# Gate bias and q spreads ahead of load issues on GpSimd, an even split of the k sort copies, MoE pieces from unit 16, and the last four q heads loaded behind the first row scatters

## The chip, the cores and the metric

The kernel runs on one core of a Trainium2 chip. A core has five engines that each run their own list of instructions in order: TensorE (PE, matrix multiplies; its weight loads are shown as PEld), VectorE (DVE), ScalarE (ACT), GpSimd (POOL, which here also issues the large loads and the indirect scatters) and SyncE (SP, which here only issues transfers). They meet through semaphores. The metric is the device time of a run in microseconds: 243.31 us as the median of three runs (243.28 to 244.02). The profiled execution has a span of 207.0 us from its first to its last instruction; times within the profile are counted from the start of that span.

## The reference

Two parts are computed, one behind the other. First a block attention with sorted blocks, for 4 batches of 8 heads, 768 positions and 64 columns per head:

```
P = sort_net (8 x 8 for each head), 5 times: exp, rows to sum 1, columns to sum 1
k_sorted, v_sorted = P applied to the 8 blocks of 96 rows of k and v
scores = q_block . k_sorted_block^T / 8    (96 x 96 per block)
attn_out = softmax(scores) . v_sorted_block
```

The result is laid out as x, 3072 rows of 512 columns. Then a mixture of experts with one expert for each row:

```
logits = x @ w_gate + modality_bias[modality_id];  e = argmax;  p = softmax(logits)[e]
out = p * (relu(x @ w1[e]) @ w2[e])       w1: 512 x 1024, w2: 1024 x 512, 8 experts
```

## The kernel before, in words

**Attention.** Heads and batches are packed into two groups g (two batches each). A group has 16 units, numbered u = 0 to 15 for group 0 and 16 to 31 for group 1: one head (u modulo 8), of two batches at once, for four of the eight blocks. For each group the blocks of k and v are sorted by matmuls with a block diagonal matrix made of P (`make_bd`); `sort_k` (L361) and `sort_v` (L371) do it in jobs, and each job's PSUM tile is copied out by ScalarE or VectorE. Which of the two is chosen by `pick` (L344): it keeps a running sum of costs for both (`busy`, charged through `use`) and gives a copy to the one with the smaller sum. The tile of a job comes from one of three pools, named "mi" (four tiles), "sc" and "op" (one tile each, twice as wide); the list `kinds` (L763) names the pool for each of the jobs of group 0. Group 1's jobs are spread over units 8 to 15.

q is loaded by head, laid side by side for two batches by a copy (`spread_q`, L123, two copies for each pair of heads, on GpSimd for group 0 and on VectorE for group 1), and transposed by TensorE (`prep_q`: tq). A unit then is `scores` (sc), `expo` (ScalarE's exp), `av` (op, and VectorE's division by the row sums into xb). `prep_s` and `prep_q` prepare q for units u + 3 and u + 2.

**Gate.** Eight units finish 768 rows of x, a stage m (0 to 3). `gate_T` transposes xb (gt), `gate_L` multiplies with w_gate (lg) and adds into lacc; its first part adds biasm, the bias of each row, which `gate_bias` (L327, four GpSimd instructions) makes. `choose` takes the argmax, `place` (L491) works out the slot of each row and sends the rows with eight indirect scatters from GpSimd to a scratch in DRAM (xs_scratch), and `table_x` works out which slots are full and loads them, transposed, on SyncE's queue.

**Experts.** Two experts' weights fit (w01). The MoE work is a list of pieces: a quarter of the first product for 256 rows (`mL1`, hp) or half of the second (`mL2`, yp, followed by an indirect scatter of rows to the output from GpSimd). `run_pieces(n)` puts the next n pieces into the order, if their rows have been asked for. `pace` (L881) says how many pieces a unit takes: none before unit 17, then one or two. After the units the rest follows.

**Order.** The order is written out by hand: what is emitted first stands first in its engine's list, and nothing behind a waiting instruction can overtake it. `at1(u, ...)` puts work in the middle of unit u (ahead of `av`), `at2(u, ...)` at its end. On GpSimd the sequence is: loads of q, k and v of group 0; spread of heads 0 and 1; loads of k of group 1; tables of the gate (`home_map`, `gate_w`, L323); spread of heads 2 and 3; load of v of group 1 (it waits until v of group 0 has been read); spread of heads 4 and 5; q of group 1 (`load_q`, L116) and the first expert's weights, in turn; small constants; spread of heads 6 and 7; the gate bias; then the rows of stage 0, the second expert's weights (`late_w1`, which waits for the transposed load of the second slot), and so on. `home_pick` (L214) is a chain of 13 small VectorE instructions that is emitted ahead of the sort of k.

Of the kernel before, what the change touches and what calls it, by code (L numbers as in the profile page):

```python
# [17 lines left out]
def kernel(  # L18
# [13 lines left out]
    nc = tc.nc  # L32
# [58 lines left out]
    def q_in(g, hh):  # L91
        base = q_in1 if g else v_sb[1].rearrange("p x d -> p (x d)")
        return base[:, hh * 3072:(hh + 1) * 3072]
# [15 lines left out]
    def load_k(g, part):  # L109
        cs = slice(part * RW // 2, (part + 1) * RW // 2)  # L110
        nc.gpsimd.dma_start(out=k_raw[:, cs], in_=k_src[g * 128:(g + 1) * 128, cs])

    def load_v(g):
        nc.gpsimd.dma_start(out=v_in, in_=v_src[g * 128:(g + 1) * 128])

    def load_q(g, h0, nh):  # L116
        t = q_in(g, h0 // 4).rearrange("p (r h f) -> p r h f", r=2, h=4)
        z = h0 % 4
        for par in range(2):
            nc.gpsimd.dma_start(out=t[:, par, z:z + nh], in_=q[2 * g + par, h0:h0 + nh]  # L120
                                .rearrange("h (p t) d -> p h (t d)", t=6))

    def spread_q(g, hq, eng=None):  # L123
        t = q_in(g, hq // 2).rearrange("p (r h t d) -> p r h t d", r=2, h=4, t=6)
        il = q_il[hq % 2].rearrange("p (h t r d) -> p h t r d", h=2, t=6, r=2)
        for z in range(2):
            (eng or nc.vector).tensor_copy(il[:, z], t[:, :, (hq % 2) * 2 + z].rearrange("p r t d -> p t r d"))  # L127
# [62 lines left out]
    def perm_mult(dst, srcs, nm):  # L190
        eng = nc.gpsimd
        tmp = small.tile([128, 4, E, E], FP32, tag="ptmp", name=f"ptmp{nm}")
        a = bass.AP(tensor=srcs.tensor, offset=srcs.offset, ap=[srcs.ap[0], srcs.ap[1], [0, E], srcs.ap[2]])
        p_ = bass.AP(tensor=perm.tensor, offset=perm.offset, ap=[perm.ap[0], [0, 4], perm.ap[1], perm.ap[2]])
        eng.tensor_tensor(tmp, a, p_, ALU.mult)
        for w in (4, 2):
            eng.tensor_tensor(tmp[:, :, :, 0:w], tmp[:, :, :, 0:w], tmp[:, :, :, w:2 * w], ALU.add)
        eng.tensor_tensor(dst.rearrange("p r (e o) -> p r e o", o=1), tmp[:, :, :, 0:1], tmp[:, :, :, 1:2], ALU.add)
# [32 lines left out]
    def tq_pe(u):  # L231
        h = u % 8
        src = q_il[(h // 2) % 2].rearrange("p (h t f) -> p h t f", h=2, t=6)[:, h % 2]
        tp = mipsum.tile([128, 6, 128], BF16, tag="mi", name=f"tq{u}")
        for t in range(6):
            nc.tensor.transpose(tp[:, t], src[:, t], ident)  # L236
        tq[u] = tp

    def tq_out(u, eng):
        g, h = u // 16, u % 8  # L240
        qT = qTb[g][:, h * 768:(h + 1) * 768].rearrange("p (i t r) -> p i t r", i=NB, t=6)
        eng(qT, tq.pop(u).rearrange("p t (i r) -> p i t r", r=16))
# [55 lines left out]
    def home_map():  # L298
        nc.vector.tensor_tensor_scan(cs_, ones8, oth, 0.0, ALU.mult, ALU.add)
        nc.vector.scalar_tensor_tensor(cs_, cs_, 1.0, oth, ALU.add, ALU.mult)  # L300
        nc.vector.tensor_tensor(cs_, cs_, ohB, ALU.add)
        hb = bass.AP(tensor=cs_.tensor, offset=cs_.offset, ap=[cs_.ap[0], [0, E], cs_.ap[1]])
        nc.vector.tensor_tensor(perm, hb, sF8.broadcast_to([128, E, E]), ALU.is_equal)
        perm_mult(BTp, BT, "b")
        nc.gpsimd.tensor_copy(etab, BTp[0:1, 3])
# [6 lines left out]
    def mod_rows():  # L312
        src = modI.rearrange("b (r t w) -> b t r w", r=16, t=6)[:, :, :, 0]
        nc.gpsimd.tensor_copy(modB, src)
# [8 lines left out]
    def gate_w():  # L323
        perm_mult(wgf, wg_sb, "w")
        nc.gpsimd.tensor_copy(wgp, wgf)

    def gate_bias():  # L327
        nc.gpsimd.tensor_scalar(modN, modF, -1.0, 1.0, ALU.mult, ALU.add)

        def bb(r):  # L330
            t = BTp[0:BLK, r]
            return bass.AP(tensor=t.tensor, offset=t.offset, ap=[t.ap[0], [0, NTL], t.ap[1]])
        tmp = small.tile([BLK, NTL, E], FP32, tag="btmp", name="btmp")
        nc.gpsimd.tensor_tensor(biasm, modF.broadcast_to([BLK, NTL, E]), bb(1), ALU.mult)
        nc.gpsimd.tensor_tensor(tmp, modN.broadcast_to([BLK, NTL, E]), bb(0), ALU.mult)
        nc.gpsimd.tensor_tensor(biasm, biasm, tmp, ALU.add)
# [3 lines left out]
    def use(act=0.0, dve=0.0):  # L340
        busy[0] += act
        busy[1] += dve

    def pick(act, dve):  # L344
        top = max(busy)
        for z in range(2):
            busy[z] = max(busy[z], top - 3.0)
        z = 0 if busy[0] + act <= busy[1] + dve else 1
        busy[z] += (act, dve)[z]
        return z == 0  # L350
# [28 lines left out]
    def jobs(g, kinds):  # L379
        res, c0, d0 = [], 0, 0  # L380
        for kd in kinds:
            if c0 < BLK:
                res.append((sort_k, g, c0, kd))
                c0 += 8 if kd == "mi" else 16
            else:
                res.append((sort_v, g, d0, kd))
                d0 += 4 if kd == "mi" else 8
        assert c0 == BLK and d0 == D
        return res
# [3 lines left out]
    def unit(u):  # L393
        return u // 16, (u // 8) % 2, u % 8
# [6 lines left out]
    def prep_q(u):  # L401
        if 2 <= u < 32 and not (u // 8) % 2:
            tq_pe(u)
            tq_out(u, nc.scalar.copy if pick(0.8, 0.56) else nc.vector.tensor_copy)
# [23 lines left out]
    def av(u):  # L428
        g, hf, h = unit(u)
        xt = xb[(u // 8) % 2]  # L430
        op = opsum.tile([128, 2, 512], FP32, tag="op", name=f"op{u}")
        ov = op[:, :, 0:4 * (D + 1)].rearrange("p r (j x) -> p r j x", x=D + 1)
        for par in range(2):
            for j in range(4):
                i = hf * 4 + j
                c0 = (par * 4 + j) * BLK
                nc.tensor.matmul(ov[:, par, j], attnT[u % 2][:, c0:c0 + 128],  # L437
                                 v_sb[g][0:BLK, par * 64 + h * 8 + i, 0:D + 1], start=True, stop=True)
        rs = small.tile([BLK, 2, 4, 1], FP32, tag="rs", name=f"rs{u}", bufs=2)
        nc.vector.reciprocal(rs, ov[0:BLK, :, :, D:D + 1])  # L440
        nc.vector.tensor_tensor(xt[:, :, h * D:(h + 1) * D].rearrange("p (r j) d -> p r j d", r=2),  # L441
                                ov[0:BLK, :, :, 0:D], rs.broadcast_to([BLK, 2, 4, D]), ALU.mult)
        use(dve=0.92)
# [171 lines left out]
    def zero_block():  # L615
        ins = nc.sync.dma_start(out=xs_dram[ZR:ZR + PR].rearrange("(t p) w -> p t w", t=2), in_=zsrc2)
        in_xs_group(ins.ins)
        pads.append(ins.ins)
# [125 lines left out]
    m_, s_, o_ = "mi", "sc", "op"  # L744
# [15 lines left out]
    use(dve=0.5)  # L760
    home_pick()
    mod_rows()
    kinds = [s_, o_] + [m_] * 8 + ([m_] * 4 + [o_]) * 2 + [m_] * 4  # L763
    g0 = jobs(0, kinds)
    for f, g, x0, kd in g0[:10]:
        f(g, x0, kd)
# [3 lines left out]
    load_k(1, 0)  # L770
    load_k(1, 1)
    home_map()
    gate_w()
    spread_q(0, 1, nc.gpsimd)
    use(dve=-busy[1], act=-busy[0])
    for n, (f, g, x0, kd) in enumerate(g0[10:]):
        f(g, x0, kd)
# [2 lines left out]
            expo(1)  # L780
    load_v(1)
    spread_q(0, 2, nc.gpsimd)
    load_q(1, 0, 4)
    load_w(0, parts=(0,))
    load_q(1, 4, 4)
    load_w(0, parts=(1,))
    make_upper_triangular(nc, maskUT, val=1.0, diag=False)
    nc.gpsimd.iota(zpad.bitcast(I32)[:, Dm // 2:Dm // 2 + 1], pattern=[[0, 1]], base=SKIP, channel_multiplier=0)
    zero_block()
    prep_q(2)  # L790
    av(0)
    prep_q(3)

    st = {"tab": -1, "x": 0, "l1": 0, "done": 0, "pos": 0}

# [21 lines left out]
    def at1(u, f, *a):  # L817
        A1.setdefault(u, []).append((f, a))

    def at2(u, f, *a):  # L820
        A2.setdefault(u, []).append((f, a))
# [7 lines left out]
    for m in range(4):  # L829
        for c in range(4):  # L830
            u = 8 * m + 2 * c + 3
# [5 lines left out]
                at1(u, gate_L, m, c)  # L837
        if m < 3:
            at1(8 * m + 9, choose, m)
    at2(2, lambda: (spread_q(0, 3, nc.gpsimd), gate_bias()))  # L840
    at2(3, make_bd, 1)
    at2(4, late_consts)
    k_at = [8] * 3 + [9] * 3 + [10] * 4 + [11] * 2
# [1 line left out]
    for u, (f, g, x0, kd) in zip(k_at + v_at, jobs(1, [m_] * 28)):  # L845
        at2(u, f, g, x0, kd)
    for m in range(3):
        at2(8 * m + 9, place, m)
        at2(8 * m + 11, table_x, m)
    at2(12, late_w1)  # L850

    PIPE = 6
# [13 lines left out]
    def run_pieces(n):  # L866
        for _ in range(n):
            if st["pos"] >= len(pieces):
                return
            f, a = pieces[st["pos"]]  # L870
            if (f is mL1 and a[0] >= st["x"]) or (f is last_L1 and SL >= st["x"]):
                return
            f(*a)
            if f is mL1 and a[1] == 3:
                st["l1"] = a[0] + 1
            if f is mL2 and a[1] == 1:
                st["done"] = a[0] + 1
            x_try()
            st["pos"] += 1

    def pace(u):  # L881
        return (0, 0) if u < 17 else (1, u % 2)

    for u in range(2, 32):
        p1, p2 = pace(u)
# [10 lines left out]
            f(*a)  # L896
    run_pieces(1)
    av(31)
    run_pieces(1)
    gate_T(3, 3)  # L900
    run_pieces(1)
    gate_L(3, 3)
    choose(3)
    run_pieces(1)
    place(3)
    run_pieces(1)
    table_x(3)
    run_pieces(1000)
    assert st["pos"] == len(pieces)
# [74 lines left out]
```

The softmax here doesn't subtract the row's maximum and nothing guards it: scores larger than these inputs give would overflow.

## Time and profile before

| engine | busy us | share of the span |
|---|---|---|
| TensorE, matmuls | 166.8 | 81% |
| TensorE, weight loads | 121.8 | 59% |
| VectorE | 102.1 | 49% |
| ScalarE | 92.6 | 45% |
| GpSimd | 83.5 | 40% |

The share of an engine is a mean over stages that differ: up to about 40 us the loads and the two sorts set the pace, then the units, and from 81 us the units together with the MoE pieces. The profile's page shows the span in 40 slices of 5.2 us, in which a digit is the busy share in tenths; "PEclk" is the clock that TensorE was granted. The order of time shows each instruction with its start, its length, its engine, its line, what it writes and reads, and in brackets how long its engine stood idle before it and what ended that. The bulk of the traffic is 23.10 MB on GpSimd's queue; 27.35 MB are read from memory and 10.52 MB written. Loads of f32 are turned into bf16 on the way.

### The profile page before, as it was taken

To read this page: it belongs to the slowest core of one execution; us is meant where nothing else is said; L and a number is where in the kernel's file an instruction comes from. 1 tells how busy PE (TensorE), PEld (TensorE's weight loads), DVE (VectorE), ACT (ScalarE), POOL (GpSimd) and SP (SyncE) were. 2 spreads that over 40 slices of the span, in tenths; PEclk is the share of its full clock that TensorE was granted. 3 is DMA by queue.
4 is the path that set the end of the run, shared out by engine and by line. 5 is a ranking of instruction groups with operands and counts; after the bars stand their busy time and mean duration, and the time that the engine had idled before them with its cause. 6 is when DMAs were issued, how large, how long until landed. Compare 5 with 4: busy or idle time off the path is not lost.

```text
span 207.0 us, 5130 instructions
## 1 busy us (share of the span) xinstructions
PE 166.8 (81%) x2034; PEld 121.8 (59%) x2045; DVE 102.1 (49%) x333; ACT 92.6 (45%) x148; POOL 83.5 (40%) x118
## 2 busy tenths in 40 slices
PE   6395497438899998999978999889999999999100
PEld 2135496327698887768657586648676767654000
DVE  5969377255484866864638453572222322223000
ACT  2035368325575797759435674434232223232000
POOL 7901377930007603177241773257631313132300
PEclk9859679755555799999999999999999999999955
DMA  4999999999993326998550226963577321212200
GB/s 54 207 228 205 194 221 196 204 186 211 205 190 81 88 54 57 165 181 215 152 153 3 77 80 184 177 172 110 165 186 187 83 103 51 101 55 101 62 2 0
DMA packets 30160, 27.66 MB, mean 134 GB/s; under 512 B 18831, under 2 KB 25775, under 8 KB 29872
## 3 DMA queue, kind: packets, MB, share of 16 engines
q0 software_dynamic: 11792, 23.10, 51.0%
q1 hardware_dynamic: 18336, 4.16, 11.3%
q8 instruction: 18, 0.29, 0.6%
q14 instruction: 14, 0.11, 0.2%
HBM read 27.35 MB, written 10.52 MB: 183 GB/s over the span
## 4 chain that ended last, share of the span: by engine, by line
PE 60%; issue 10%; POOL 9%; DVE 9%; DMA 4%; ACT 2%; POOLq 0%; DVEq 0%
PE yp L706 20%; PE hp L683 18%; PE gt L450 4%; DMA kvb<-in_k_dram 4%; PE sc L418 3%; PE lg L456 3%; PE op L437 3%; PE ka L366 3%; DVE xb L441 2%; POOL q_il L127 2%; PE va L375 2%; POOL q_in L120 1%; ACT v_sb L353 1%; PE tq L236 1%; PE ypl L736 1%
## 5 line engine op out<-in xcount | busy, mean ns | idle before, releaser
L683 PE MATMUL hp<-xT,w 128*128 128x256 bf16 x384 | 47.3, 273 | 0.1
L527 POOL DMA_INDIRECT xs_scratch<-xb,dest x32 | 29.6, 926 | 38.8 <-issue 37.9
L697 POOL DMA_INDIRECT out_dram<-kvb,idg x25 | 24.5, 982 | 42.9 <-DVE kvb L695 22.0
L683 PEld LDWEIGHTS <-w 128*128 128x128 bf16 x384 | 36.1, 98 | 7.4
L424 ACT ACTIVATE attnT<-sc 96x768 bf16<-96x768 f32 x32 | 25.9, 808 | 10.4 <-PE sc L418 10.1
L441 DVE TENSOR_TENSOR xb<-op,rs 96x512 bf16<-96x512 f32 x32 | 22.0, 686 | 1.2
L706 PE MATMUL yp<-w,qT 128*128 128x512 bf16 x91 | 22.3, 380 | 0.3
L706 PE MATMUL yp<-w,hT 128*128 128x512 bf16 x90 | 21.9, 380 | 0.3
L693 ACT ACTIVATE kvb<-yp,idg 128x512 f32<-128x512 f32 x14 | 9.6, 687 | 20.5 <-PE yp L706 20.5
L695 DVE TENSOR_SCALAR kvb<-yp,idg 128x512 f32<-128x512 f32 x10 | 7.5, 751 | 19.1 <-PE yp L706 17.2
L437 PE MATMUL op<-v_sb,attnT 96*128 96x65 bf16 x256 | 14.9, 206 | 0.7 <-DVE xb L441 0.4
L677 ACT ACTIVATE hT<-hp 128x512 bf16<-128x512 f32 x17 | 10.1, 594 | 11.5 <-PE hp L683 11.2
L450 PE MATMUL gt<-ident,xb 96*128 96x96 bf16 x128 | 9.4, 225 | 7.2 <-DVE xb L441 6.8
L677 ACT ACTIVATE qT<-hp 128x512 bf16<-128x512 f32 x15 | 9.0, 597 | 12.4 <-PE hp L683 12.1
L706 PEld LDWEIGHTS <-hT 128*128 128x128 bf16 x96 | 9.0, 98 | 9.0
L706 PEld LDWEIGHTS <-qT 128*128 128x128 bf16 x96 | 9.1, 98 | 9.0
L437 PEld LDWEIGHTS <-attnT 96*128 96x128 bf16 x256 | 12.3, 106 | 2.8 <-DVE xb L441 0.6
L418 PE MATMUL sc<-qT,kT 64*128 64x96 bf16 (+1 forms) x256 | 12.8, 226 | 1.3 <-ACT kT L353 0.7
L236 PE MATMUL tq<-ident,q_il 128*128 128x128 bf16 x96 | 9.2, 242 | 5.7 <-POOL q_il L127 5.7
L375 PE MATMUL va<-bd,kvb 128*128 128x128 bf16 x128 | 13.8, 278 | 0.0
L366 PE MATMUL ka<-bd,kvb 128*64 128x64 bf16 x384 | 10.0, 220 | 4.3 <-issue 2.0
L375 PEld LDWEIGHTS <-kvb 128*128 128x128 bf16 x128 | 12.8, 191 | 0.3
(179 smaller groups left out, 225.6 us busy)
## 6 DMA issues: line engine op xcount, KB each, us to landing
w<-in_moe_w_dram POOLq DMA_DIRECT2D x4, 1024.0 KB, 8.3
kvb<-in_k_dram POOLq DMA_DIRECT2D x4, 768.0 KB, 9.6
kvb<-in_v_dram POOLq DMA_DIRECT2D x2, 1536.0 KB
q_in<-in_q_dram POOLq DMA_DIRECT2D x4, 384.0 KB, 21.4
xs_scratch<-zpad SPq DMA_DIRECT2D x3, 258.0 KB, 3.3
v_sb<-in_q_dram POOLq DMA_DIRECT2D x4, 192.0 KB, 4.1
v_sb<-in_q_dram POOLq DMA_DIRECT2D x2, 384.0 KB, 21.5
xs_scratch<-xb,dest POOLq DMA_INDIRECT x32, 2.4
```

Source lines behind the costliest of these rows:

```text
L366: nc.tensor.matmul(acc[par * 64:(par + 1) * 64, z], k_raw[:, (c0 + z) * D:(c0 + z + 1) * D], bd[g][:, par * 64:(par + 1) * 64], start=True ...
L375: nc.tensor.matmul(acc[:, z], v_cols[:, d0 + z], bd[g], start=True, stop=True)
L418: nc.tensor.matmul(sc[0:m, par, j * BLK:(j + 1) * BLK], kT[g][rows, x0:x0 + m], qT[rows, i], start=True, stop=True)
L424: mark[0] = nc.scalar.activation(attnT[u % 2][:, 0:8 * BLK].rearrange("p (r f) -> p r f", r=2), sc_tiles.pop(u)[0:BLK, :, 0:4 * BLK], ACT. ...
L437: nc.tensor.matmul(ov[:, par, j], attnT[u % 2][:, c0:c0 + 128], v_sb[g][0:BLK, par * 64 + h * 8 + i, 0:D + 1], start=True, stop=True)
L441: nc.vector.tensor_tensor(xt[:, :, h * D:(h + 1) * D].rearrange("p (r j) d -> p r j d", r=2), ov[0:BLK, :, :, 0:D], rs.broadcast_to([BLK, ...
L450: nc.tensor.transpose(tp[:, t], xb[m % 2][:, t, c * 128:(c + 1) * 128], ident[:BLK, :BLK])
L527: ins = nc.gpsimd.indirect_dma_start(out=xs_dram, out_offset=bass.IndirectOffsetOnAxis(ap=dest[:, t:t + 1], axis=0), in_=xt.bitcast(I32)[: ...
L677: mark[0] = nc.scalar.activation(dst, src, ACT.Relu)
L683: nc.tensor.matmul(hp[:, f], w_at(s, c * F + (2 * j + f) * 128, 128), xT_b[s % NX][:, c], start=(c == 0), stop=(c == 3))
L697: ins = nc.gpsimd.indirect_dma_start(out=out, out_offset=bass.IndirectOffsetOnAxis(ap=idg[:, t, 0:1], axis=0), in_=y, in_offset=None, boun ...
L706: nc.tensor.matmul(yp, hT_b[s % 2][:, fc, t * 128:(t + 1) * 128], w_at(s, 4 * F + fc * Dm, Dm), start=(fc == 0), stop=(fc == 7))
```

## The change

The change moves work in the hand-written order and alters none of the results.

- The cost sum of VectorE is charged 1.6 us more before the sort of k of group 0, and the wide "op" job stands sixth instead of second in the list, so that ScalarE and VectorE get five copies each, where ScalarE had six and VectorE four. It is meant to take account of home_pick, which VectorE works off first.
- On GpSimd the spread of heads 2 and 3 goes ahead of `gate_w`, and the gate bias and the spread of heads 6 and 7 go ahead of the load issues of q and of the weights, whose data is needed later.
- The last four q heads of group 1 are no longer loaded between the halves of the weights, but behind the scatters of stage 0, at the end of unit 10.
- Pieces begin in unit 16 instead of 17. In the tail three calls take two pieces in place of one, and the placing of stage 2 moves from the end of unit 25 into unit 26.

```diff
-    kinds = [s_, o_] + [m_] * 8 + ([m_] * 4 + [o_]) * 2 + [m_] * 4
+    use(dve=1.6)
+    kinds = [s_] + [m_] * 4 + [o_] + [m_] * 4 + ([m_] * 4 + [o_]) * 2 + [m_] * 4
...
     home_map()
+    spread_q(0, 1, nc.gpsimd)
     gate_w()
-    spread_q(0, 1, nc.gpsimd)
...
     load_v(1)
     spread_q(0, 2, nc.gpsimd)
+    gate_bias()
+    prep_q(2)
+    av(0)
+    prep_q(3)
+    spread_q(0, 3, nc.gpsimd)
     load_q(1, 0, 4)
     load_w(0, parts=(0,))
-    load_q(1, 4, 4)
     load_w(0, parts=(1,))
...
-    prep_q(2)
-    av(0)
-    prep_q(3)
...
-    at2(2, lambda: (spread_q(0, 3, nc.gpsimd), gate_bias()))
...
     for m in range(3):
-        at2(8 * m + 9, place, m)
+        if m == 2:
+            at1(26, place, m)
+        else:
+            at2(8 * m + 9, place, m)
         at2(8 * m + 11, table_x, m)
+    at2(10, load_q, 1, 4, 4)
     at2(12, late_w1)
...
     def pace(u):
-        return (0, 0) if u < 17 else (1, u % 2)
+        return (0, 0) if u < 16 else (1, u % 2)
...
     run_pieces(1)
     av(31)
-    run_pieces(1)
+    run_pieces(2)
     gate_T(3, 3)
     run_pieces(1)
     gate_L(3, 3)
     choose(3)
-    run_pieces(1)
+    run_pieces(2)
     place(3)
-    run_pieces(1)
+    run_pieces(2)
     table_x(3)
```

## The prediction

> **What bounds the kernel now.** I read the page first. TensorE is busy for 81% of the span, and the chain that ended last is 60% TensorE, so most of the span is TensorE's. What can be won cheaply is therefore where TensorE stands still or runs at half clock. In the page's 40 slices (5.2 us each) both show at one place:
>
> ```profile
> PE   6395497438899998999978999889999999999100
> PEclk9859679755555799999999999999999999999955
> DMA  4999999999993326998550226963577321212200
> ```
>
> In the seventh slice PE still has 7 tenths, then 4 and 3; the granted clock falls in the eighth and is at half for five slices from the ninth, while PE is back at 8 and 9 tenths. DMA is full for twelve slices. The list of waits names the causes:
>
> ```profile
> DVE lacc L462 <- POOL biasm L336: 6.0, 1, 6.0
> ...
> PE gt L450 <- DVE xb L441: 6.8, 5, 3.5
> ...
> PE tq L236 <- POOL q_il L127: 5.7, 2, 3.2
> ```
>
> The columns are total us, times and longest. VectorE waits once, for 6.0 us, for the gate bias that GpSimd makes. Now the order of time on GpSimd and TensorE there (start, length):
>
> ```profile
> 32.84 1.60 POOL L127 COPY q_il<-v_sb 128x768 bf16<-128x768 bf16 x2
> 34.37 1.50 POOL L120 DMA_DIRECT2D q_in<-in_q_dram  x2
> 35.86 0.76 POOL L638 DMA_DIRECT2D w<-in_moe_w_dram  x1
> 36.59 1.51 POOL L120 DMA_DIRECT2D q_in<-in_q_dram  x2
> 38.05 0.93 POOL L640 DMA_DIRECT2D w<-in_moe_w_dram  x1
> ...
> 39.61 1.58 POOL L127 COPY q_il<-v_sb 128x768 bf16<-128x768 bf16 x2
> ...
> 42.65 0.72 POOL L336 TENSOR_TENSOR biasm<-biasm,btmp 96x256 f32<-96x256 f32 x1
> ```
>
> ```profile
> 37.51 0.42 PE L437 MATMUL op<-v_sb,attnT 96*128 96x65 bf16 x8
> 40.48 0.82 PE L236 MATMUL tq<-ident,q_il 128*128 128x128 bf16 x6 [2.55 <-POOL q_il L127]
> 41.23 0.50 PE L418 MATMUL sc<-qT,kT 64*128 64x96 bf16 x8
> 45.23 0.82 PE L450 MATMUL gt<-ident,xb 96*128 96x96 bf16 x8 [3.49 <-DVE xb L441]
> ```
>
> GpSimd spends 34.37 to 39.0 on issuing loads and only then spreads the last q heads and makes the bias. TensorE waits 2.55 us for the spread. Then it waits 3.49 us for xb of unit 3, which VectorE could have made from 37.9 (its matmuls ended) but makes at 44.48, because the add of the bias (43.40) stands ahead of it. Its matmuls before the gap take 0.42 us, those after it 0.62 for the same work. The next fact is at the other end, the first rows of the MoE:
>
> ```profile
> 61.83 1.05 POOL L527 DMA_INDIRECT xs_scratch<-xb,dest  x1 [15.12 <-issue]
> ...
> 81.12 0.85 POOL L638 DMA_DIRECT2D w<-in_moe_w_dram  x1 [9.64 <-DMA xT<-xs_scratch]
> ```
>
> ```profile
> 73.39 1.36 SPq L650 DMA_TRANSPOSE xT<-xs_scratch  x1
> ```
>
> The first row scatter starts at 61.83, the first transposed load at 73.39, which with the page's median 3.4 us has landed at 76.8, 15.0 us after the first scatter. The first hp matmul starts at 81.15 and stands only behind the code's own order (unit 17); from there to the last matmul at 192.3 TensorE has 95% of the time.
>
> **What the Trainium skill says.** "TensorE: Matmul & The Clock Gate", What's actually happening: the clock is either full or half, set by free-running windows of 3.4 us, half after an idle one, full after a busy one. The trace agrees on states and grid: read us by us, the clock changes at 8.5, 15.3, 22.1, 29.0, 39.2 and 69.9, all on one grid of 3.41 us. But the window that lost it (35.8 to 39.2) had TensorE busy 2.06 us of 3.4, and the one before kept it with 2.44; so "idle" is too strong, and the border lies between. Windows at half clock with 3.34 and 3.19 busy did not bring it back. Same page, Architectural detail: VectorE and ScalarE take instructions strictly in order, GpSimd too. The trace agrees: xb above. "DMA: Bandwidth & Descriptors", Queues, rings and completion order: an engine works off one queue in ring order and takes turns between queues. The trace agrees with the first half: v_sb loads issued at 5.5 to 8.3 landed 21.5 us later, behind k and v. How a Pool load and a SyncE transpose share the engines no row here shows.
>
> **The change, part by part.**
> 1. Bias and last spread ahead of the load issues. The spread of heads 4 and 5 ends at 34.44 as before. The bias takes 43.37 − 41.18 = 2.19 us, so it is there at 36.6; the gate logits are there at 37.2. The 6.0 us wait goes to nothing. The last spread's first half (0.8 us) ends at 37.4; its transposes come up at 37.93. The 2.55 wait goes too. With VectorE free at 37.4: add 0.2, group 1's sort matrix 0.9, xb 0.9, so xb at 39.2 and the gate transpose there instead of at 45.23: **−6.0 us**. What the moved issues delay is hidden: the 1.5 MB of v issued at 32.25 keep the engines full to about 40 (at 200 GB/s), and q and w issued at 38.2 instead of 34.4 queue behind it.
> 2. The clock. TensorE does not stand still, so the window to 39.2 gains the transposes and scores of 0.68 us, 2.7 of 3.4, more than the 2.44 that kept the clock. From the gate transpose (45.23) to the sort of group 1 (54.82) are 9.6 us now. At full clock the rows shrink to about 0.63 (0.82 to 0.52, 0.62 to 0.41, 0.50 to 0.34); 8.0 us busy would save 3.0, but xb chains fill some: bounds 0 and 3.0, I take **−2.5**. From 54.82 to 69.9 TensorE is busy 14.7 us at half clock; all of it at full saves 5.4, and ScalarE with 7.4 of 10 us busy cannot follow that far; bounds 0 and 5.4, I take the middle, **−2.7**. Unit 16 then comes 11.2 us early.
> 3. First pieces a unit earlier, and the last four q heads behind the first scatters. Rows leave 9.3 us earlier (6.0, 2.5, and 0.8 of the 2.7 that lie ahead of them): first scatter 52.5, first rows at 67.5. Unit 16's scores go from 78.71 to 67.5: the first piece comes up just as its rows land. But the q load of 0.79 MB is now issued at 62.3 behind eight scatters of 1.2 us, moves for 3.9 us at 200 GB/s, and shares engines with the transposes. It delays the rows by 0 (turns) to 3.9 us (all ahead): **+2.0**. On GpSimd two issues (1.5 us) come ahead of the second expert's w, which waits for rows at that time anyway: nothing. The heads are used for unit 20, prepared in unit 17, at 69 or later; they land at 67 or so: nothing.
> 4. Two pieces at a time in the tail. TensorE stands still 0.68 and 0.70 us at 133.5 and 135.5 and slows around: 0 to 1.4, I take **−0.7**. The later scatter (unit 26 rather than 25) and two more output scatters ahead of the last rows cost nothing: these rows are at 151 (147.58 and 3.4), and some 16 pieces of about 1.75 us lie between the new last scatter and their first use.
> 5. Even k sort evacuations: VectorE goes from 4 to 5 copies, ScalarE from 6 to 5, and home_pick, which keeps VectorE until 18.76, no longer holds a 16-column job. TensorE waits 1.34 us for it and then 1.96 us for nothing shown (inside one job, which this edit can't cure). Bounds 0 and 1.9; **−0.5**. The spread of heads 2 and 3 ahead of gate_w: not waited for today, nothing.
>
> Sum: −6.0 −2.5 −2.7 +2.0 −0.7 −0.5 = −10.4. The timed runs stand some 36 us above the span (243.3 against 207.0) and I carry the difference over one for one: 243.3 − 10.4 = **232.9 us**.
>
> **The rivals.** *Clock lost again.* Units 6 and 7 have no q transposes left; a window then holds some 2.4 us busy, on the border. If it goes at 42.6 or 46.0, step 2 is −1.5 and the group 1 sort runs as now: −6.0 −1.5 +0.1 −0.7 −0.5 = −8.6: 234.7 (rows with the load's 2.0 at 71.3, unit 16 at 71.2). For: the narrow border, and that 3.3 us busy did not bring it back. Against: xb comes sooner and packs units. *Only the standstill goes.* The window to 39.2 loses the clock as before and later waits move into units 5 to 9, so steps 2, 4 and 5 bring nothing: −6.0: 237.3. *Everything earlier, nothing waits.* The q load slips between the transposes (step 3 costs 0), and steps 4 and 5 bring their upper bounds: −6.0 −2.5 −2.7 −1.4 −1.9 = −14.5: 228.8. For: rows at 67.5 and unit 16 move together. *Slower.* The late q load lands after unit 17's spread and VectorE, in order, stops; rows and second expert slip behind it; TensorE cools, and units 16 to 21, some 16 us, run at half speed. Half speed costs up to 0.6 of 16, 9.6 us, the wait 3.9: 13.5 against 11.2 + 1.2 won: 244.4. For: the only new wait that can stop three engines. Against: the load has 5 us to land and DMA is at 2 to 3 tenths there.
>
> **How the numbers follow.** Forecast 42%; clock lost again 33%; only the standstill 8%; everything earlier 12%; slower 5%. The range has to hold forecast, clock lost and part of each neighbour: step 3's 0 to 3.9 puts ±2 on the forecast, step 2's bounds 3; 228.5 to 237.5 leaves out the slow case and the tails of the −6.0 and −14.5 cases. Faster 0.94, within 0.3% 0.02, slower 0.04.
>
> **What would show it.** Right: no wait of VectorE on biasm, TensorE's idle between 37.9 and 45 under 1 us, clock full in the ninth slice, first scatter at 52 to 54, first hp at 67 to 71. Step 2 wrong: the clock at half again before the group 1 sort. Step 3 wrong: hp's first wait on xT over 4 us, or VectorE waiting on q_in at L127. It would be wrong as a whole if the bias, in its new place, came later than 37.2 because GpSimd waits for load_v's release longer than until 32.25.

## The result, and the profile after

The changed kernel took 236.81 us (median of four runs, 235.57 to 238.71), the kernel before 243.52 us beside it: a ratio of 0.9729, with a 95% interval of 0.9658 to 0.9799. The forecast was 232.9 us, its range 228.5 to 237.5, so direction and range held. The experiments show that the sum behind the number was wrong in three terms which partly cancelled, and that the gain depends on the chip.

One thing has to be known before two pages are compared. The page of before, with its span of 207.0 us, and the 243.3 us of its timed runs are not the same situation. The kernel before took 206.0 and 206.2 us on two of the chips used below, and 245.0 and 245.1 us on two others. The page of the changed kernel is from a chip of the long kind, its span is 233.9 us. Two of the pages below, of the changed kernel in the second group and of the later rows in the third, are from executions 0.8% and 0.5% longer than the median of their runs. The slices of the changed kernel's page (5.8 us each) show what the short pages don't have:

```profile
PE   6573988695289899229989129999659999999400
...
PEclk9799599757559999857999758999959999999965
DMA  5999999999396696242111255404436431211200
```

There are four holes in TensorE's row, at slices 11, 17 and 18, 23 and 24, and 29 and 30, and the clock falls in or behind each. The list of waits says who stood still (total us, times, longest):

```profile
ACT attnT L424 <- remote: 19.6, 3, 9.2
...
PE sc L418 <- ACT attnT L424: 15.7, 5, 8.9
...
PE lg L456 <- issue: 5.4, 1, 5.4
...
PE tq L236 <- POOL q_il L127: 2.9, 1, 2.9
```

"Remote" means that no row of the profile ended the wait. This page holds 1,110 records of landed transfers, the pages of the short kind some 1,700, so the row may also be one that was not recorded. The order of time puts the holes beside the row scatters of the four stages. For stage 2, GpSimd's last rows and ScalarE:

```profile
133.54 0.91 POOL L527 DMA_INDIRECT xs_scratch<-xb,dest  x1 [0.30 <-issue]
134.76 1.00 POOL L697 DMA_INDIRECT out_dram<-kvb,idg  x1 [0.30 <-issue]
136.06 0.98 POOL L697 DMA_INDIRECT out_dram<-kvb,idg  x1 [0.30 <-issue]
```

```profile
137.85 0.81 ACT L424 ACTIVATE attnT<-sc 96x768 bf16<-96x768 f32 x1 [9.19 <-remote]
```

The scores that this exp reads were done at 128.6, the scatters ran from 125.0 to 137.0, and ScalarE goes on 0.8 us after the last.

On GpSimd the change does what it was meant to do: VectorE's wait for biasm is gone from the list, the one wait left for q_il is at 9.6 us, before the sort, and the places that were shown of before now read

```profile
32.18 1.60 POOL L127 COPY q_il<-v_sb 128x768 bf16<-128x768 bf16 x2
...
35.23 0.72 POOL L336 TENSOR_TENSOR biasm<-biasm,btmp 96x256 f32<-96x256 f32 x1
35.90 1.58 POOL L127 COPY q_il<-v_sb 128x768 bf16<-128x768 bf16 x2
37.44 1.60 POOL L120 DMA_DIRECT2D q_in<-in_q_dram  x2
39.03 0.75 POOL L638 DMA_DIRECT2D w<-in_moe_w_dram  x1
39.77 0.91 POOL L640 DMA_DIRECT2D w<-in_moe_w_dram  x1
```

```profile
37.87 0.35 PE L418 MATMUL sc<-qT,kT 64*128 64x96 bf16 x8 [0.27 <-ACT attnT L424]
38.53 0.51 PE L450 MATMUL gt<-ident,xb 96*128 96x96 bf16 x8 [0.31 <-DVE xb L441]
...
42.63 0.41 PE L437 MATMUL op<-v_sb,attnT 96*128 96x65 bf16 x8
43.44 0.80 PE L456 MATMUL lg<-wgp,xTg 128*96 128x8 bf16 x8 [0.40 <-DVE xTg L353]
44.18 0.50 PE L418 MATMUL sc<-qT,kT 64*128 64x96 bf16 x8
44.61 0.62 PE L437 MATMUL op<-v_sb,attnT 96*128 96x65 bf16 x8
```

The second gate transposes start at 38.53 instead of 45.23. But in the last line the same matmuls (op) take 0.62 us where they had taken 0.41: the granted clock is at half again from 43.3, before the sort of group 1 (47.0). The first scatter leaves at 54.02 (61.83 in the page of before, which is of the short kind), the first transposed load is issued at 69.72 and the first piece starts at 78.92 (81.15). Of the 7.8 us won at the scatter 2.2 are left at the first piece. On this chip the hole at slice 11 lies between the two; how much of the loss is the late q load needs the experiments.

### The profile page after: what moved, and what is told of

The parts are those of the page before. It is cut to its first block, busy times and chain, and to the rows that moved or that the text cites. A ratio compares the mean times of both kernels' runs of the same rounds, so it can differ in the third digit from the quotient of the medians.

```text
span 233.9 us, 5147 instructions
## 1 busy us (share of the span) xinstructions
PE 170.7 (73%) x2045; PEld 123.5 (53%) x2045; DVE 102.3 (44%) x333; ACT 93.0 (40%) x148; POOL 83.6 (36%) x118
## 4 chain that ended last, share of the span: by engine, by line
PE 59%; DVE 14%; another core or an unknown queue 9%; issue 6%; ACT 3%; POOL 1%; POOLq 0%; DVEq 0%; ACTq 0%
PE yp L706 18%; PE hp L683 17%; PE va L375 5%; PE sc L418 3%; PE op L437 3%; PE gt L450 3%; DVE xb L441 3%; PE ka L366 3%; PE lg L456 3%; ACT attnT L424 1%; DVE P_t L272 1%; DVE kT L353 1%; DVE hT L675 1%; ACT v_sb L353 1%
## 5 line engine op out<-in xcount | busy, mean ns | idle before, releaser
L683 PE MATMUL hp<-xT,w 128*128 128x256 bf16 x384 | 49.9, 282 | 0.5 <-ACT hT L677 0.5
L683 PEld LDWEIGHTS <-w 128*128 128x128 bf16 x384 | 37.3, 101 | 9.8 <-issue 1.8
L706 PE MATMUL yp<-w,qT 128*128 128x512 bf16 x96 | 24.4, 400 | 4.6 <-ACT hT L677 4.6
L418 PE MATMUL sc<-qT,kT 64*128 64x96 bf16 (+1 forms) x256 | 12.7, 224 | 17.0 <-ACT attnT L424 15.7
L706 PE MATMUL yp<-w,hT 128*128 128x512 bf16 x96 | 22.5, 379 | 0.0
L418 PEld LDWEIGHTS <-kT 64*128 64x128 bf16 (+1 forms) x256 | 7.8, 103 | 19.3 <-issue 17.6
L695 DVE TENSOR_SCALAR kvb<-yp,idg 128x512 f32<-128x512 f32 x11 | 8.3, 750 | 22.0 <-PE yp L706 22.0
L677 ACT ACTIVATE qT<-hp 128x512 bf16<-128x512 f32 x16 | 9.5, 596 | 17.9 <-PE hp L683 16.7
L440 DVE RECIPROCAL rs<-op 96x8 f32<-96x8 f32 x32 | 6.3, 198 | 22.9 <-remote 7.4
L693 ACT ACTIVATE kvb<-yp,idg 128x512 f32<-128x512 f32 x13 | 8.9, 687 | 17.8 <-PE yp L706 15.7
L456 PE MATMUL lg<-wgp,xTg 128*96 128x8 bf16 x128 | 8.9, 193 | 6.7 <-issue 5.4
```

The source lines that it names most:

```text
L418: nc.tensor.matmul(sc[0:m, par, j * BLK:(j + 1) * BLK], kT[g][rows, x0:x0 + m], qT[rows, i], start=True, stop=True)
L456: nc.tensor.matmul(lg[:, t], xTg[c % 2][:, t], wgp[:, c], start=True, stop=True)
L677: mark[0] = nc.scalar.activation(dst, src, ACT.Relu)
L683: nc.tensor.matmul(hp[:, f], w_at(s, c * F + (2 * j + f) * 128, 128), xT_b[s % NX][:, c], start=(c == 0), stop=(c == 3))
L706: nc.tensor.matmul(yp, hT_b[s % 2][:, fc, t * 128:(t + 1) * 128], w_at(s, 4 * F + fc * Dm, Dm), start=(fc == 0), stop=(fc == 7))
```

## The experiments

Twelve runs were made in four groups, each group on one chip of its own; every ratio is to the kernel before on the same chip. The kernel before took 206.23 us beside the first group, 244.98 beside the second, 205.99 beside the third and 245.11 beside the last.

**The kernel before, unchanged.**

> The kernel before, unchanged, run again with its profile beside the changed kernel's. What is open: the page of before showed a span of 207.0 us where its timed runs took 243.3, and the changed kernel's page shows 233.9 with waits of 5 to 9 us on ScalarE, VectorE and TensorE that no row explains (releaser 'another core or an unknown queue'), each beside a run of row scatters on GpSimd. Theory A (waits of this kind are in both kernels, and the first page of before happened to have none): the time is 243.3 to 244.0 again and a new page has a span near 241 with 30 us or more of such waits during the four scatter stages. Theory B (they are new in the changed kernel and ate part of its gain): a new page of before has a span near 207 without them.

Measured: 205.94 us, ratio 0.9983 (0.9960 to 1.0005), span of the page 205.3, with a single wait of 1.8 us on "remote". Neither theory is decided, as the time itself was 38 us lower: the page and the time agree here, so the first page of before was no accident of one execution, and the 36 us that I had carried over as if fixed come and go with the chip (or with the time at which it ran, which was not separated).

**Part 1 alone.**

```diff
     spread_q(0, 2, nc.gpsimd)
+    gate_bias()
+    prep_q(2)
+    av(0)
+    prep_q(3)
+    spread_q(0, 3, nc.gpsimd)
     load_q(1, 0, 4)
...
-    at2(2, lambda: (spread_q(0, 3, nc.gpsimd), gate_bias()))
```

(The three preparation lines leave their place behind `zero_block`.)

> Part 1 alone: on GpSimd the gate bias and the spread of heads 6 and 7 stand ahead of the load issues, all else as before. My theory: part 1 takes away the standstill of 6.0 us and, with it, some half-clock time, so it alone brings most of the gain: ratio 0.965 to 0.975, about 235 to 237.5 us. Rival (the gain comes from the later q load and the earlier pieces): ratio 0.99 or above.

Measured: 198.92 us, 0.9638 (0.9600 to 0.9677). Part 1 alone wins 7.5 us, more than the whole change wins on this kind of chip (below). The second gate transposes in the page of the kernel before on the same chip, and then TensorE's order of time in this page:

```profile
44.63 0.82 PE L450 MATMUL gt<-ident,xb 96*128 96x96 bf16 x8 [3.50 <-DVE xb L441]
```

```profile
38.37 0.52 PE L450 MATMUL gt<-ident,xb 96*128 96x96 bf16 x8 [0.31 <-DVE xb L441]
38.72 0.41 PE L437 MATMUL op<-v_sb,attnT 96*128 96x65 bf16 x8
...
42.12 0.82 PE L450 MATMUL gt<-ident,xb 96*128 96x96 bf16 x8
42.74 0.64 PE L437 MATMUL op<-v_sb,attnT 96*128 96x65 bf16 x8
```

Against the page of before the second gate transposes are 6.3 us earlier (44.63 to 38.37), the sort of group 1 7.1 (54.23 to 47.15), the first piece 7.5 (79.31 to 71.81) and the last matmul 7.4 (190.49 to 183.06). So the standstill is worth 6.3, and at most 1.2 is left for the clock: it is lost again at 41.6, and the transposes go from 0.52 to 0.82 within one unit.

**All but part 1.**

```diff
     spread_q(0, 2, nc.gpsimd)
-    gate_bias()
-    prep_q(2)
-    av(0)
-    prep_q(3)
-    spread_q(0, 3, nc.gpsimd)
     load_q(1, 0, 4)
...
+    at2(2, lambda: (spread_q(0, 3, nc.gpsimd), gate_bias()))
```

(The three preparation lines go back behind `zero_block`.)

> The changed kernel with part 1 undone: bias and last spread behind the load issues again, all other edits kept. My theory: nearly nothing is left, 0.990 to 1.000 of before (241 to 243.5 us), as the standstill is back. Rival (the other parts carry the gain): 0.975 to 0.985.

Measured: 210.37 us, 1.0184 (1.0146 to 1.0223). Both expectations missed: the other edits together don't do nothing, they cost 3.8 us. Below the old wait for xb, TensorE's list shows one that the kernel before does not have, for the rows of the first piece:

```profile
PE gt L450 <- DVE xb L441: 6.8, 7, 3.7
PE hp L683 <- DMA xT<-xs_scratch: 5.5, 2, 4.6
```

The first piece waits 4.6 us for its rows, which come 19.4 us after the first scatter (78.91 and 59.52); the kernel before starts its first piece 18.1 us after (79.31 and 61.24), with no wait in front of it.

**The changed kernel with the q load early**, in the first group and again in the third, beside the changed kernel itself.

```diff
     load_w(0, parts=(0,))
+    load_q(1, 4, 4)
     load_w(0, parts=(1,))
...
-    at2(10, load_q, 1, 4, 4)
```

> The changed kernel with the load of the last four q heads back between the halves of the weights. My theory (the late load costs up to 2 us where it shares the engines with the first rows): 0 to 2 us faster than the changed kernel, ratio 0.965 to 0.973. Rival (the late load is what helps, as the first scatters no longer queue behind 0.79 MB): slower than the changed kernel by 1 to 4 us, ratio 0.977 to 0.99.

> The changed kernel once more, beside its version with the early q load on the same chip. On a chip where the kernel before takes 206 us (the first four runs): 0.970 to 0.982, with a first hp wait on xT of 2 to 5 us. On one where it takes 243 to 245: 0.960 to 0.975 as in the last four runs, with the unexplained waits beside the row scatters.

> The changed kernel with the last q heads loaded between the halves of the weights. My theory: the late load delays the first rows (19.4 us after the first scatter with it, 15.0 without), so without it the kernel is 1 to 3.5 us faster than the changed kernel on either kind of chip. Rival (on a chip with the unexplained waits the first rows are late anyway, and the later load frees the engines for the first scatters): no faster, or slower.

Measured: with the early load 200.02 us, 0.9679 (0.9635 to 0.9724), and again 199.72 us, 0.9685 (0.9641 to 0.9729). The changed kernel beside the second of these: 204.35 us, 0.9902 (0.9871 to 0.9933), smaller a gain than I expected. The late load costs 0.0217 of 206 us, 4.5 us, also more than the 1 to 3.5 expected; both runs with the early load were on chips of the short kind, so the other kind is not tested here. The first piece, with the late load and then with the early one:

```profile
71.06 0.34 PE L418 MATMUL sc<-qT,kT 64*128 64x96 bf16 x8
72.90 1.03 PE L683 MATMUL hp<-xT,w 128*128 128x256 bf16 x8 [1.50 <-DMA xT<-xs_scratch]
```

```profile
69.18 0.34 PE L418 MATMUL sc<-qT,kT 64*128 64x96 bf16 x8
69.50 1.03 PE L683 MATMUL hp<-xT,w 128*128 128x256 bf16 x8
```

From the first scatter (54.02 and 53.76) to the first piece it is 18.9 us against 15.7. SyncE's queue shows one half of how: the first transposed load is issued at 66.73 in the one and 65.19 in the other, with the last scatter issued at 62.72 and 62.46.

```profile
66.73 1.36 SPq L650 DMA_TRANSPOSE xT<-xs_scratch  x1
```

```profile
65.19 1.36 SPq L650 DMA_TRANSPOSE xT<-xs_scratch  x1
```

So the first transposed load, which has to wait for the scattered rows, is issued 4.0 us behind the last scatter instead of 2.7. The rest is in the load itself, which landed 6.0 us after its issue against 4.2. From the last scatter to this landing it is 10.0 us with the late load and 6.9 without. The first group repeats it on another chip: 10.5 us in the kernel without part 1, which has the late load, and 6.8 with the early load.

Not all of the 3.4 us between the two first pieces (72.90 and 69.50) stands in the list as a wait for rows, which is 1.5 us. TensorE was already 1.9 us behind at the scores of unit 16 (71.06 and 69.18), mainly because the clock had been at half from 57.0 to 63.8 in the one page, before the late load was issued at 63.64. Since the rows landed only at 72.8 with the late load (69.4 without), the first piece could not have come earlier in any case.

**The changed kernel on a chip where before takes 245 us, and three parts undone there.**

> The changed kernel, unchanged, beside the kernel before on this chip. My theory after the first four runs: part 1 brings 7 us, and the late q load takes part of it back, since it held the first rows to 19.4 us after the first scatter in the run with part 1 undone (15.0 before): 0.970 to 0.982, about 200 to 202.5 us where before takes 206.2, and a first hp wait on xT of 2 to 5 us. Rival (part 1's gain stays whole and the tail and the sort add to it): 0.955 to 0.965. The waits of 5 to 9 us with no row behind them, seen in the page of the changed kernel at first, are expected to be absent here as in all four runs so far; if they are there, they belong to the change.

Measured: 236.29 us, 0.9622 (0.9572 to 0.9672). The chip was of the other kind than the expectation had in mind, and the unexplained waits are there: 22.5 us in three on attnT alone, up to 9.9. By my words ahead of the run they would then belong to the change; the third group (g0, the same kernel, no such wait) shows that the change alone does not bring them.

```diff
-        return (0, 0) if u < 16 else (1, u % 2)
+        return (0, 0) if u < 17 else (1, u % 2)
```

> The changed kernel with pieces from unit 17 again. My theory: the first rows land late, so the first piece in unit 16 only brings the wait forward; with unit 17 TensorE does unit 16's attention work in that time: 0.5 to 2.5 us faster than the changed kernel. Rival (the earlier piece fills idle time): 0.5 to 1 us slower than the changed kernel.

Measured: 237.11 us, 0.9655 (0.9605 to 0.9705). The intervals overlap, so neither expectation is borne out: the unit in which the pieces begin is not shown to matter here.

```diff
-        if m == 2:
-            at1(26, place, m)
-        else:
-            at2(8 * m + 9, place, m)
+        at2(8 * m + 9, place, m)
...
-    run_pieces(2)
+    run_pieces(1)
```

(The last two lines three times.)

> The changed kernel with the tail as before: one piece at a time and the placing of stage 2 at the end of unit 25. My theory (the double pieces fill TensorE's waits of 0.68 and 0.70 us): 0.3 to 1.4 us slower than the changed kernel. Rival (the waits are hidden or move to the rows of the last slots): no difference within 0.3 us.

Measured: 241.61 us, 0.9807 (0.9752 to 0.9863): 4.5 us slower than the changed kernel, three times the most I expected. The double pieces and the placing of stage 2 were undone together; the placing hardly moved that stage's first scatter (125.25 and 125.09), which speaks for the pieces. How they may pay is seen in the two pages. With double pieces TensorE resumes like this beside and behind the scatters of stage 3, and with single ones like the second fence:

```profile
168.88 1.03 PE L683 MATMUL hp<-xT,w 128*128 128x256 bf16 x8 [0.52 <-issue]
174.53 3.57 PE L706 MATMUL yp<-w,qT 128*128 128x512 bf16 x8 [4.61 <-ACT hT L677]
```

```profile
170.35 1.87 PE L683 MATMUL hp<-xT,w 128*128 128x256 bf16 x8 [4.00 <-issue]
175.41 3.57 PE L706 MATMUL yp<-w,qT 128*128 128x512 bf16 x8 [3.19 <-ACT qT L677]
```

They come out of the hole within 0.9 us of each other, but the last matmul ends at 221.84 in the one and 225.97 in the other: the kernel with double pieces has three pieces more (16 hp and 8 yp matmuls) behind it when it goes into the hole.

```diff
-    use(dve=1.6)
-    kinds = [s_] + [m_] * 4 + [o_] + [m_] * 4 + ([m_] * 4 + [o_]) * 2 + [m_] * 4
+    kinds = [s_, o_] + [m_] * 8 + ([m_] * 4 + [o_]) * 2 + [m_] * 4
...
-    spread_q(0, 1, nc.gpsimd)
     gate_w()
+    spread_q(0, 1, nc.gpsimd)
```

> The changed kernel with the k sort copies split 6 to 4 as before and the gate tables ahead of the spread of heads 2 and 3. My theory (the wait for a copy of 1.34 us goes, but TensorE then stands longer at the wait with no row behind it in the same sort, 3.27 against 1.51 us): within 0.5 us of the changed kernel. Rival (the even split is worth its 1.3 us and more): 1 to 2 us slower than the changed kernel.

Measured: 236.86 us, 0.9668 (0.9616 to 0.9720), not told apart from the changed kernel. In the pages of the third group's changed kernel and of this one, the changed split and then the old one:

```profile
19.21 0.63 PE L366 MATMUL ka<-bd,kvb 128*64 128x64 bf16 x28 [0.21 <-DVE kT L353]
22.21 0.25 PE L366 MATMUL ka<-bd,kvb 128*64 128x64 bf16 x4 [2.37 <-issue]
```

```profile
20.45 0.63 PE L366 MATMUL ka<-bd,kvb 128*64 128x64 bf16 x28 [1.34 <-DVE kT L353]
22.21 0.32 PE L366 MATMUL ka<-bd,kvb 128*64 128x64 bf16 x4 [1.14 <-issue]
```

The wait for a copy shrinks by 1.1 us, the wait in the middle of the next job grows by 1.2, and both continue at 22.21. What ends that wait the profile does not show; it came no earlier although the copy did.

The name "even split" does not fit what ran. The copies of this sort in the page of the changed kernel:

```profile
16.51 3.89 ACT L353 CAST kT<-ka 128x1024 bf16<-128x1024 f32 x6 [2.66 <-PE ka L366]
18.47 1.88 DVE L353 CAST kT<-ka 128x512 bf16<-128x512 f32 x3
...
22.50 0.69 DVE L353 CAST kT<-ka 128x512 bf16<-128x512 f32 x1 [2.15 <-PE ka L366]
```

ScalarE still has six copies and VectorE four, not five each. What moved is the second wide copy, from VectorE (1.22 us in the old order) to ScalarE (1.06 us). So TensorE waits less because VectorE's first narrow copy no longer stands behind home_pick and a wide copy, not because the copies are evenly divided.

**Rows of stage 1 three units later, in the kernel before.**

```diff
-        at2(8 * m + 9, place, m)
-        at2(8 * m + 11, table_x, m)
+        at2(8 * m + 9 + 3 * (m == 1), place, m)
+        at2(8 * m + 11 + 3 * (m == 1), table_x, m)
```

> The kernel before with only the rows of stage 1 placed and scattered three units later (end of unit 20, table in unit 22). It serves two questions. Whether the kernel before also has the unexplained waits of ScalarE, VectorE and TensorE where it takes 243 us: theory A says yes, 30 us or more in all, rival B says none. And whether they follow the row scatters: theory A says the wait of stage 1 moves by some 8 to 10 us with its scatters and ends as they end; rival C (they belong to a place in the program or to the clock time, as a fetch of instructions would) says it stays in units 19 to 22. On a chip without such waits: within 1% of before, as rows of slots 2 and 3 have little slack.

Measured: 212.31 us, 1.0270 (1.0228 to 1.0312), on a chip without the waits, so neither of its two questions was answered. It shows something else: moving a scatter back by three units costs 5.6 us, with a wait of 4.3 us of hp on xT. My "within 1%" was wrong; the rows of slots 2 and 3 have no three units of slack.

**Part 1 and the tail, without the rest**, as a version that might beat both.

```diff
-        at2(8 * m + 9, place, m)
+        if m == 2:
+            at1(26, place, m)
+        else:
+            at2(8 * m + 9, place, m)
...
-    run_pieces(1)
+    run_pieces(2)
```

(On top of part 1 alone; the last two lines three times.)

> The kernel before with part 1 and the tail's double pieces only: no late q load, pieces from unit 17, the k sort as before. It is the candidate for a version that beats both. On a chip where before takes 206 us: my theory (the tail fills waits of 0.7 us each) 0.958 to 0.962, 0.3 to 1.2 us better than part 1 alone (0.9638); rival (the tail's gain was bound to the unexplained waits) 0.963 to 0.967. On a chip where before takes 243 to 245: 0.940 to 0.960 if the late q load costs there too (the changed kernel had 0.962 to 0.973), 0.960 or above if it does not.

Measured: 235.55 us, 0.9617 (0.9579 to 0.9655), on a chip with the waits, level with the changed kernel's 0.9622 on another such chip (in the result it had 0.9729, so comparisons between chips are no finer than that). It is just above the 0.960 that I had named as the border, with an interval on both sides of it. So there the late q load, the earlier pieces and the change of the copies bring or cost little together; the late load alone was not tested there. The pages show why it could be cheap: in this one and in that of f0 the first piece follows the scores ahead of it without a wait for rows (at 80.97 and at 79.08, in unit 17 and in unit 16). The hole beside the scatters has made TensorE late, so that the rows are in time even with the late load. Whether this version beats part 1 alone on a chip without the waits was not measured.

## Why the prediction was right, and where it was not

**Step 1, the standstill (−6.0): right.** Part 1 alone brings the second gate transposes forward by 6.3 us, with the bias ready at 35.8, ahead of the logits, as worked out. Undone in the changed kernel it costs 0.028 between two chips of the short kind (1.0184 and 0.9902), 5.8 us.

**Step 2, the clock (−2.5 and −2.7): mis-sized, at most 1.2 us in place of 5.2.** The step failed where it took it that the work behind the standstill would keep the full clock. The first window behind it did, the next one did not: the rival "clock lost again", which I gave 33%, is what happened, at 40.3 to 43.5 us in every page with part 1, and so did the sign that I had named, half clock before the sort of group 1. The reason I gave against it, that units pack closer, was too weak. The border that I had read off, between 2.06 us of busy TensorE in a window and 2.44, was none. In the third group's page of the changed kernel, whose changes of the clock lie on a grid of 3.41 us too, the first of these two windows lost the clock and the second kept it (behind the stretch: its length, then busy us of PE; the granted share is the third number from the end):

```profile
39.94:43.36 3.42, 2.32 (x48) 1.86 (x48) 2.35 (x8) 2.29 (x3) 1.46 (x5) 1.00 0.94 170
70.67:74.08 3.41, 1.92 (x31) 1.64 (x30) 1.06 (x4) 1.64 (x3) 0.00 (x0) 1.00 0.98 125
```

Behind the first the clock is at half from 43.36, behind the second it stays full to 190.1. In the page of the kernel with the old k sort (f3) a window with 2.52 lost it. So the busy time of one window does not tell what happens, and what does is open. A second reason lies in the page that I started from: it got the full clock back at 69.9, the page of the same kernel in the first group at 63.3, in the middle of group 1's sorts, so that part of the −2.7 was a loss that the kernel before need not have.

**Step 3, the late q load (+2.0, bounds 0 and 3.9): right that it delays the rows, mis-sized.** It is +4.5 us on a chip without the waits. Of the Trainium skill's turn-taking between queues ("DMA: Bandwidth & Descriptors", Queues, rings and completion order) I took half the transfer as the price; the rows landed 3.1 to 3.7 us later behind the last scatter, close to my other bound, the whole transfer of 3.9 us. That this comes from sharing the DMA engines is argued from the later landings; no run isolates it. My sign for it, a wait of hp of over 4 us, did not come in the changed kernel (1.5 us), as the half clock had made TensorE late too. The other side of the step, that the heads land in time for unit 17, held: VectorE's spreads ran without a long wait.

**Step 4, the tail (−0.7): not tested alone on chips without the waits, −4.5 on one with them.** The mechanism there, read from the two pages, is one I did not have: more pieces are done before the other engines stand.

**Step 5, the even split (−0.5): nothing.** I had named the wait inside one job as what this edit can't cure, and it took over what the edit freed. That VectorE goes from 4 to 5 copies was wrong as well: it kept four, and only lost the wide one.

**The carried difference: wrong as an argument.** I took some 36 us between the timed runs and the span as fixed. In the changed kernel they show as waits in the middle of the execution, on some chips, and they change what other terms are worth. On chips without them the whole change is worth 2.0 us (0.9902). It divides into part 1 −7.5, late load +4.5, and the other edits with the early load +1.0 (0.9685 against 0.9638, with intervals that overlap); the three are differences along one row of kernels, so they add up by construction and are no proof of the sum. Taken out of the changed kernel, part 1 was worth 5.8, so the parts don't simply add. On chips with the waits the change is worth 6.6 to 9.3 (0.9729 and 0.9622), and the tail's 4.5 is the only part measured alone there. Part 1's 7.5 (from the other kind of chip) and this 4.5 would make 12.0, where the kernel with both won 9.4 on a chip with the waits, so the sum does not close there. That 232.9 lay only 4 us off is therefore in part luck: step 2 was too large by 4.0 and the tail too small by 3.8, each measured on a different kind of chip. The rival's 234.7 was nearer, and its account of the clock is the one that came.

A reading to put right, on which nothing rests: DMA is full in eleven of the slices shown, not twelve.

**What stays open.** What the waits are. In all six pages from the long kind of chip ScalarE stands, but for single instructions, from within the row scatters of each stage until about 1 to 3 us after the last of these transfers is issued, and in none of the eight pages from the short kind. That makes the scatters a likely partner, and no more: no run on such a chip moved or thinned them. The same six pages hold 1,110 to 1,160 records of landed transfers against 1,705 to 1,728, so what ended these waits may be missing from them, and whether the missing records and the waits have one cause is open too. The kernel before has no page from there, so that it too has these waits is concluded from its 245 us against 206 alone.

## What to carry to other kernels

Small work on an in-order queue belongs ahead of bulk issues if another in-order engine waits for its result; here that single swap carried the gain on a chip without the waits (7.5 of 206 us), and it is read off the list of waits by looking for a short producer behind long issues. A load moved out of a full stretch is not free where it lands: behind the scatters it moved while the rows were on their way that the next stage waits for. Do not add the cure of a half clock to the cure of the standstill before it: here the clock was lost again 3 to 5 us later. And count in the trace whether a balance of two engines that the source intends is the one that ran.

## What the runs showed of the hardware

The kernel before took 206 us on two chips and 245 on two others. The changed kernel, which took 204 us on one of the former and 236 on one of the latter, had engines standing, for up to 9.9 us at a time, beside indirect scatters only on the latter. TensorE's clock was lost in windows of 3.41 us in which it was busy 2.07 us (kernel before), 2.33 (part 1 alone) and 2.52 (the old k sort in the changed kernel), and was kept in one with 1.92 (the changed kernel): busy time alone did not decide. In the page of part 1 alone the full clock is back at 55.2, within the sort of group 1. Two transposed loads that took 4.2 and 3.3 us to land took 6.0 and 4.2 when 0.79 MB of loads was issued about 3 us ahead of the first.
